# Maxout FFN behind a light convolution: the first blocks' whole-array products reordered, a conv copy moved ahead of a weight copy, three maxima taken in SBUF

## The chip, the cores and the metric

The kernel runs on one core of one Trainium2 chip. The metric is the device time of one execution in microseconds (us), as the median of several runs.

## The reference

Two steps follow each other. The first is a causal depthwise convolution over 7 positions: the 192 channels form 8 heads of 24, each head has its own 7 weights, and these go through a softmax. The second is a maxout feed-forward layer on the 33,280 resulting tokens.

```
w    = softmax(weight, axis=-1)                     # 8 heads x 7
y    = conv over 7 positions, left padded           # (8, 4160, 192) -> 33280 tokens x 192
h    = max(max(y @ w1, y @ w2), y @ w3)             # 33280 x 768
out  = h @ w_out                                    # 33280 x 192
```

## The kernel before

The 33,280 tokens are cut into 65 blocks of 512. A block's hidden layer is worked out in 6 chunks of 128 of the 768 hidden columns. The kernel uses the identity max(a, b, c) = c + max(a - c, b - c, 0): it forms the differences w1 - w3 and w2 - w3 once (`make_wd`, L320, into `wd`), takes `h = max(relu(y @ (w1-w3)), y @ (w2-w3))` for each chunk (`top`, L508 on ScalarE for the relu, L509 on VectorE for the max), and adds y @ (w3 @ w_out) at the end with a product matrix `m16` that is made once from `w3` and `w_out` (`cast_w3`, `transpose_w3`, `make_m`).

A token has 192 values, one and a half times the 128 rows of the matmul array. So each product with a difference matrix is split. The first 128 rows are one whole-array matmul, called F here. The last 64 rows are a half-array matmul, called H; the H of w1 - w3 and that of w2 - w3 stand in the two halves of the array and run side by side. Index 0 and 1 of `wd` hold the first 128 rows of the two differences, index 2 holds the last 64 rows of both, and index 3 (`cross_wd`, L331) holds copies of rows in the other half, for the form that all blocks from block 2 on use (`l1`, L521). For index 2 the last 64 rows of `w3` are needed in both halves of the partitions. They are loaded into the lower half (L244) and copied to the upper one (`copy_w3`, L324).

The weights arrive in DMAs on SyncE's queue, in three groups of 256 columns, that is two chunks each: `load_wa` (L229) brings the first 128 rows of w3, w1 and w2, `load_wb` (L233) the last 64 rows. Behind them come w_out and the inputs of blocks 2 to 6 (`load_x`, L167). Some input buffers are zeroed in part beforehand (`zero_x`, L140 on ScalarE, L137 on GpSimd or VectorE).

Blocks 0 to 3 have a conv of their own (`conv_dense`, matmuls at L396): two PSUM tiles per block, one for the 128 rows that F reads and one for the 64 rows (in both halves) that H reads, each copied to SBUF at L401 by the engine that the call names. `order=(1, 0)` works out the H tile first.

Blocks 0 and 1 run their chunks in pairs: `l1_dense` (L544) issues the F and H matmuls of two chunks, `tops` the maxima. The string "FH" or "HF" gives the order. Block 0 uses the PSUM pools `psp` and `psq` (tiles `lp` and `lq`, two banks each), block 1 uses `psw` (tiles `lw`, four banks). All engines work their instructions off in the order of the program, and a manual schedule fixes that order. `h` of block 0 then goes into the output product (`first_hidden`, L616; `first_rest`, L624 and L629; copies at L632), block 2's conv follows with its copies of halves (`cross`, L407), and from block 2 on a steady pattern interleaves `l1` (L521), the output product `st2` (L585) and the convs of later blocks.

The relus and their copies are in tiles `r` of the pool `rp` (4 buffers before).

Of the kernel before, what the change touches and what calls it, by code (L numbers as in the profile page):

```python
# [10 lines left out]
FP32 = mybir.dt.float32  # L11
FP16 = mybir.dt.float16
# [3 lines left out]
P = 128  # L16
# [5 lines left out]
NBLK = 512  # L22
CHK = 103
HALF = P // 2
# [4 lines left out]
def kernel(  # L29
# [12 lines left out]
    nc = tc.nc  # L42
    ctx.enter_context(tc.manual_schedule())

    B, SEQ, D = x.shape
    H, KWs = weight.shape
# [55 lines left out]
    ysp = ctx.enter_context(tc.tile_pool(name="ysp", bufs=2))  # L102
    ydp = ctx.enter_context(tc.tile_pool(name="ydp", bufs=4))
    ypp = ctx.enter_context(tc.tile_pool(name="ypp", bufs=5))
    rp = ctx.enter_context(tc.tile_pool(name="rp", bufs=4))
    hp = ctx.enter_context(tc.tile_pool(name="hp", bufs=2))
    tp = ctx.enter_context(tc.tile_pool(name="tp", bufs=2))
    outp = ctx.enter_context(tc.tile_pool(name="outp", bufs=3))
# [12 lines left out]
    def get_x(t):  # L121

        if not 0 <= t < NB or t in xin:
            return
        if t < XBUF:
            xbuf.append(const.tile([P, NR, D], FP32, name=f"xf_{t}"))
        xf = xbuf[t % XBUF if t < NDENSE + XBUF else NDENSE + (t - NDENSE - XBUF) % 3]
        assert all(v[0] is not xf for v in xin.values())
        xin[t] = [xf, 0, ()]

    def zero_x(t, q0=0, q1=NR, eng=None):

        if t >= NDENSE:
            get_x(t)
        xf = xbuf[t]
        if eng is not None:
            eng.memset(xf[TOK:HALF, q0:q1, :], 0.0)  # L137
            return
        zero = idle[TOK:HALF, 0:D]
        nc.scalar.copy(out=xf[TOK:HALF, q0:q1, :],  # L140
                       in_=bass.AP(tensor=zero.tensor, offset=zero.offset,
                                   ap=[list(zero.ap[0]), [0, q1 - q0], [1, D]]))
# [59 lines left out]
    NC, NSLOT, CYC = D // HALF, D // 32, 96  # L202
# [21 lines left out]
    ws, w3s = wall[:, 0:NC, :], wall[:, NC:NC + 2, :]  # L224
    PW = 2 * P

    def load_wa(f):
        for st, n, wsrc in ((w3s, 0, moe_w3), (ws, 0, moe_w1), (ws, 1, moe_w2)):
            nc.sync.dma_start(out=st[:, n, f], in_=wsrc[0:P, f])  # L229

    def load_wb(f):
        for st, lo, n, wsrc in ((ws, 0, 2, moe_w1), (ws, HALF, 2, moe_w2)):
            nc.sync.dma_start(out=st[lo:lo + HALF, n, f], in_=wsrc[P:D, f])  # L233

    wk = const.tile([NHEAD, SMALL], FP32, name="wk")[:, 0:KW]
# [5 lines left out]
    load_x(0)  # L241
    load_x(1)
    load_wa(slice(0, PW))
    nc.sync.dma_start(out=w3s[0:HALF, 1, :], in_=moe_w3[P:D, :])  # L244
    load_wb(slice(0, PW))
    for t in range(2, NDENSE):
        get_x(t)
# [39 lines left out]
    for lo, hi, copy in ((0, CUT, nc.scalar.copy), (CUT, WIN, nc.vector.tensor_copy)):  # L287
        bps = psq.tile([32, hi - lo + 3, NHEAD], FP32, tag="q", name=f"band_{lo}")
        for c in range(lo, hi):

            nc.tensor.matmul(bps[:, c - lo:c - lo + 4, :].rearrange("p c h -> p (c h)"),
                             lhsT=line[:, WIN - 1 - c:WIN + 31 - c],
                             rhs=ident16[:, 0:4 * NHEAD], start=True, stop=True)
        bands_.append((lo, hi, copy, bps))
    keep_warm((NBLK, NBLK, P), psp, "p")
    for h0, h1 in ((5, NHEAD), (0, 5)):
        for lo, hi, copy, bps in bands_:
            for a in range(4):
                copy(out=band[32 * a:32 * a + 32, h0:h1, 32 * a + lo:32 * a + hi],
                     in_=bps[:, 0:hi - lo, h0:h1].rearrange("p c h -> p h c"))  # L300
# [12 lines left out]
    wd = const.tile([P, NC + 1, DFF], FP16)  # L313
# [4 lines left out]
    def make_wd(n, j0, j1, eng=nc.vector):  # L318
        f = slice(P * j0, P * j1)
        eng.tensor_sub(out=wd[:, n, f], in0=ws[:, n, f], in1=w3s[:, n // 2, f])  # L320

    def copy_w3(copy, j0, j1):
        f = slice(P * j0, P * j1)
        copy(out=w3s[HALF:P, 1, f], in_=w3s[0:HALF, 1, f])  # L324
# [35 lines left out]
    dense, hs, outs, halves, convs, done = {}, {}, {}, {}, {}, {}  # L360
# [23 lines left out]
    def conv_dense(t, copies, pools=((None, None),) * 2, order=(0, 1)):  # L384


        yd = dense[t] = ydp.tile([P, NC, NBLK], FP16, tag="yd", name=f"yd_{t}")
        for n in order:
            slots_ = ((0, 1, 2, 3), (4, 5, 4, 5))[n]
            pool, tag = pools[n]  # L390
            ps = (pool or psw).tile([P, NBLK], FP32, tag=tag or "w", name=f"D{n}_{t}")
            for (q, b, row_lo, rlen, lo, hi, cc) in chunks_of[t]:
                for v in range(2):
                    for g, s in enumerate(slots_):
                        h = (32 * s + 31 * v) // GRP
                        nc.tensor.matmul(  # L396
                            ps[32 * g:32 * g + 32, lo:hi],
                            lhsT=xz[t][v][0:rlen, q, 32 * s:32 * s + 32],
                            rhs=band[0:rlen, h, cc:cc + hi - lo],
                            start=(v == 0), stop=(v == 1), tile_position=(0, 32 * g))  # L400
            copies[n](out=yd[:, 2 * n, :], in_=ps[:])  # L401
# [46 lines left out]
    def y_row(t, i):  # L448
        return dense[t][HALF * i:HALF * (i + 1), 0, 0, 0, 0, :]

    def y_all(t, i, c):
        if t < NDENSE:
            return dense[t][HALF * i:HALF * (i + 1), side(i, c), :]
        a = y_row(t, i)
        s0, s1, s2, s3 = (spot(t, i, c, r) for r in range(4))
        assert s3 - s2 == s1 - s0
        return bass.AP(tensor=a.tensor, offset=a.offset + P * s0,
                       ap=[list(a.ap[0]), [P * (s2 - s0), 2], [P * (s1 - s0), 2], [1, P]])
# [42 lines left out]
        assert not ops  # L501
        clock[0] = clock[1] = 0

    def top(t, j, ps):
        if t not in hs:
            hs[t] = hp.tile([P, NJ, NBLK], FP16, tag="h", name=f"h_{t}")
        r = rp.tile([P, NBLK], FP16, tag="r", name=f"r_{t}_{j}")
        nc.scalar.activation(out=r[:], in_=ps[0][:], func=AF.Relu)  # L508
        nc.vector.tensor_max(out=hs[t][:, j, :], in0=r[:], in1=ps[1][:])  # L509
        done[t] = j + 1  # L510

    def l1(t, j, pools=((psp, "p"), (psq, "q"))):
# [18 lines left out]
    def l1_dense(tiles, parts="FH"):  # L531

        meet()
        for n, part in enumerate(parts):
            for t, j, pools in tiles:
                for i, (pool, tag) in enumerate(pools):
                    if (t, j, i) not in open_ps:
                        open_ps[t, j, i] = pool.tile([P, NBLK], FP32, tag=tag, name=f"l{tag}{i}_{t}_{j}")
                        begun.discard((t, j, i))
                    if part == "F":  # L540
                        a, b = wd[:, i, P * j:P * (j + 1)], dense[t][:, 0, :]
                    else:
                        a, b = w_of(i, NC - 1, j), y_all(t, i, NC - 1)
                    nc.tensor.matmul(open_ps[t, j, i][:], lhsT=a, rhs=b,  # L544
                                     start=(t, j, i) not in begun, stop=(t, j, i) in begun)
                    begun.add((t, j, i))

    def tops(*tiles):
        for t, j in tiles:
            top(t, j, (open_ps[t, j, 0], open_ps[t, j, 1]))  # L550

    open_ps, begun = {}, set()

# [143 lines left out]
    zero_x(5, eng=nc.gpsimd)  # L697
    make_wd(0, 0, 2)
    make_wd(1, 0, 2)
    copy_w3(ACT, 0, 2)  # L700
    make_wd(2, 0, 2)
    conv_dense(1, (DVE, ACT), order=(1, 0))
    copy_w3(ACT, 2, 6)
    for n in range(NC):
        make_wd(n, 2, 4, nc.gpsimd)
    for n in range(NC):
        make_wd(n, 4, 6, nc.gpsimd)
    cast_w3(0, 6)
    GP(out=wo[:], in_=wos[:])
    l1_dense([(0, 0, PQ), (0, 1, PQ)], "F")  # L710
    l1_dense([(0, 0, PQ), (0, 1, PQ)], "H")
    tops((0, 0), (0, 1))
    l1_dense([(1, 0, WW), (1, 1, WW)], "HF")
    tops((1, 0), (1, 1))
    zero_x(6)
    for t in range(NDENSE, XBUF):
        load_x(t)
    l1_dense([(0, 2, PQ), (0, 3, PQ)], "FH")
    tops((0, 2), (0, 3))
    l1_dense([(1, 2, WW), (1, 3, WW)], "HF")  # L720
    tops((1, 2), (1, 3))
    cross_wd(0, ACT)
    l1_dense([(0, 4, PQ), (0, 5, PQ)], "FH")
    tops((0, 4), (0, 5))
    cast_dense(2, (GP, GP))
# [1 line left out]
    tops((1, 4), (1, 5))  # L727
    transpose_w3((PQ[0], PQ[0], PQ[1]))
    cast_dense(3, (GP, GP))
    cross_wd(1, ACT)  # L730
    first_hidden(0)
    first_hidden(1)
# [118 lines left out]
```

## Time and profile before

| | before |
|---|---|
| median of 3 runs | 452.76 us (452.75 to 453.1) |
| profiled execution, its own time | 454.16 us |
| its span, first to last instruction | 452.40 us |
| PE busy | 445.5 us (98%) |
| VectorE (DVE) busy | 354.6 us (78%) |
| ScalarE (ACT) busy | 320.2 us (71%) |
| GpSimd (POOL) busy | 207.6 us (46%) |
| granted TensorE clock | 1.00 |

Busy time is a mean over stages that have different limits, so the table says only that PE is the busiest. The change touches the first 25 us alone; its cost has to be read from that stretch: which wait ends last in front of PE, and how long the stretch is up to the point from which PE never waits again. PE is matmuls, PEld weight loads into the array, SP (or SPq) SyncE's queue. An entry in brackets behind a row is the idle time of that engine just before it, and what released it.

### The profile page before, as it was taken

How to read it: one execution, taken by the hardware profiler on the slowest of the kernel's cores; microseconds unless marked ns; L12 is line 12 of the kernel's file. 1: busy time of each engine (PE TensorE's matmuls, PEld its weight loads, DVE VectorE, ACT ScalarE, POOL GpSimd, SP SyncE). 2: the span in 40 equal slices, each digit the busy share in tenths (PEclk: the TensorE clock that was granted, in tenths of full speed). 3: DMA queues.
4: the chain of work that ended last, by engine and by line, in shares of the span. 5: the costliest groups of instructions: out<-in, count | busy, mean ns of one | idle time of the engine just before them, and what ended most of it. 6: DMA issues, size and time to landing. Idle time of an engine off the chain costs nothing.

```text
span 452.4 us, 18264 instructions
## 1 busy us (share of the span) xinstructions
PE 445.5 (98%) x7576; PEld 409.8 (91%) x7576; DVE 354.6 (78%) x607; ACT 320.2 (71%) x601; POOL 207.6 (46%) x239
## 2 busy tenths in 40 slices
PE   7999999999999999999999999999999999999997
PEld 4469999999999989999999999999999999999996
DVE  6668787878878787787887787887887887887775
ACT  6967767767777677676676776777776776776664
POOL 5864836556463533724824635525533644224000
PEclk9999999999999999999999999999999999999999
DMA  7968987696885659649649748657649668152123
GB/s 197 239 181 167 203 186 197 155 217 171 170 220 147 165 137 205 162 121 199 167 127 198 178 110 191 191 114 193 178 112 197 172 157 143 54 136 75 58 71 106
DMA packets 128163, 72.01 MB, mean 159 GB/s; under 512 B 52305, under 2 KB 127888, under 8 KB 128080
## 3 DMA queue, kind: packets, MB, share of 16 engines
q1 hardware_dynamic: 127919, 70.75, 65.9%
q8 instruction: 59, 0.97, 0.9%
q14 instruction: 25, 0.20, 0.2%
q10 hardware_dynamic: 160, 0.10, 0.1%
HBM read 33.28 MB, written 25.56 MB: 130 GB/s over the span
## 4 chain that ended last, share of the span: by engine, by line
PE 96%; DMA 1%; ACT 1%; SPq 1%; issue 1%; DVE 0%; ACTq 0%
PE po L585 36%; PE lq L521 32%; PE lp L521 22%; PE G L375 3%; DMA wall<-in_moe_w_dram 1%; ACT r L508 1%; PE D L396 1%; PE po L643 0%; PE po L616 0%; PE lw L544 0%; SPq L229 0%; SPq L167 0%; PE pm L355 0%; ACT wall L324 0%; PE lq L544 0%
## 5 line engine op out<-in xcount | busy, mean ns | idle before, releaser
L585 PE MATMUL po<-wo,h 64*128 64x192 f16 x3024 | 331.7, 243 | 0.0
L509 DVE TENSOR_TENSOR h<-r,lq 128x512 f16<-128x512 f16 x384 | 263.0, 686 | 86.2 <-ACT r L508 76.3
L508 ACT ACTIVATE r<-lp 128x512 f16<-128x512 f32 x384 | 228.9, 597 | 113.8 <-PE lp L521 103.0
L521 PE MATMUL lp<-yp,wd 64*128 64x512 f16 x1098 | 295.6, 376 | 0.0
L521 PE MATMUL lq<-yp,wd 64*128 64x512 f16 x1098 | 295.5, 376 | 0.0
L585 PEld LDWEIGHTS <-h 64*128 64x128 f16 x3024 | 242.7, 94 | 5.4 <-issue 4.1
L521 PEld LDWEIGHTS <-wd 64*128 64x128 f16 x2268 | 181.7, 94 | 14.8 <-issue 0.2
L199 POOL CAST x<-xf 103x768 f16<-103x768 f32 x122 | 97.3, 825 | 114.4 <-DMA xf<-in_x_dram 99.6
L585 PE MATMUL po<-m,yp 64*128 64x192 f16 x720 | 140.3, 243 | 0.0
L438 POOL COPY yp<-yp 64x1536 f16<-64x1536 f16 (+1 forms) x70 | 90.9, 1298 | 86.0 <-DMA yp<-ys 49.1
L593 DVE TENSOR_TENSOR o<-a,po 128x384 f32<-128x384 f32 x126 | 69.0, 547 | 0.0
L585 PEld LDWEIGHTS <-yp 64*128 64x128 f16 x720 | 66.3, 94 | 0.1
L592 ACT COPY a<-po 128x384 f32<-128x384 f32 x126 | 59.6, 473 | 0.0
L415 ACT CAST ys<-G 128x480 f16<-128x480 f32 (+1 forms) x53 | 25.4, 530 | 9.5 <-PE G L375 9.2
L415 DVE CAST ys<-G 128x480 f16<-128x480 f32 (+1 forms) x53 | 30.1, 610 | 0.0
L375 PE MATMUL G<-x,band 39*32 39x240 f16 (+3 forms) x1024 | 16.5, 242 | 0.0
L375 PEld LDWEIGHTS <-band 39*32 39x32 f16 x1024 | 10.2, 92 | 4.6 <-issue 4.1
L521 PE MATMUL lq<-yd,wd 64*128 64x512 f16 x36 | 9.7, 376 | 0.0
L521 PE MATMUL lp<-yd,wd 64*128 64x512 f16 x36 | 9.7, 376 | 0.0
L544 PEld LDWEIGHTS <-wd 128*128 128x128 f16 (+1 forms) x48 | 3.0, 95 | 7.3 <-issue 1.7
L396 PEld LDWEIGHTS <-xz 112*32 112x32 f16 x320 | 4.1, 96 | 2.9 <-issue 1.4
L216 POOL CAST xz<-xf 112x160 f16<-112x160 f32 (+2 forms) x18 | 5.1, 328 | 3.2 <-DMA xf<-in_x_dram 3.0
(75 smaller groups left out, 100.0 us busy)
## 6 DMA issues: line engine op xcount, KB each, us to landing
xf<-in_x_dram SPq DMA_DIRECT2D x113, 234.0 KB
out_dram<-o SPq DMA_DIRECT2D x62, 384.0 KB
xf<-in_x_dram SPq DMA_DIRECT2D x7, 204.8 KB
wall<-in_moe_w_dram SPq DMA_DIRECT2D x11, 128.0 KB
xf<-in_x_dram SPq DMA_DIRECT2D x3, 420.0 KB
yp<-ys SPq DMA_TRANSPOSE x70
out_dram<-o SPq DMA_DIRECT2D x5, 192.0 KB
wos<-in_moe_w_out_dram SPq DMA_DIRECT2D x1, 576.0 KB
```

The lines of the kernel that those rows point to most:

```text
L199: nc.gpsimd.tensor_copy(out=x16s[t0][0:K, :, :, u, r, :].rearrange("p h j c -> p j h c"), in_=xf[0:K, 4 * r:4 * r + 4, :].rearrange("p j ( ...
L216: copy(out=xz[t][v][0:rl, q0:q1, :].rearrange("p q (k c) -> p q k c", c=CYC)[:, :, :, a:b], in_=xf[0:rl, q0:q1, :].rearrange("p q (k c) -> ...
L375: nc.tensor.matmul(G[2 * (k // per) + i][TOK * j:TOK * (j + 1), k % per, :], lhsT=band[row, h, HALF * i + LAP:HALF * i + KR], rhs=x16s[t0] ...
L396: nc.tensor.matmul(ps[32 * g:32 * g + 32, lo:hi], lhsT=xz[t][v][0:rlen, q, 32 * s:32 * s + 32], rhs=band[0:rlen, h, cc:cc + hi - lo], star ...
L415: copy(out=slots[t][:, i % 2, :, :, GRP * h0:GRP * (h0 + per)].rearrange("p u r (h c) -> p h (u r) c", c=GRP), in_=G[i][:].rearrange("p h ...
L438: nc.gpsimd.tensor_copy(out=yp[HALF * i:HALF * (i + 1), 1, :, :, :, :].rearrange("p i u k n -> p (i u k n)"), in_=yp[HALF * (1 - i):HALF * ...
L508: nc.scalar.activation(out=r[:], in_=ps[0][:], func=AF.Relu)
L509: nc.vector.tensor_max(out=hs[t][:, j, :], in0=r[:], in1=ps[1][:])
L521: nc.tensor.matmul(ps[i][:], lhsT=w_of(i, c, j), rhs=y_all(t, i, c), start=(n == 0), stop=(n == NC - 1))
L585: nc.tensor.matmul(ps[b0, i][:, s % 2, :], lhsT=a, rhs=b, start=first, stop=last)
L592: nc.scalar.copy(out=a[:], in_=ps[s - 1, 0][:])
L593: nc.vector.tensor_add(out=outs[t][:, s - 1:s + 1, :], in0=a[:], in1=ps[s - 1, 1][:])
```

## The change

- `l1_dense` with "F" takes the two chunks' products with w1 - w3 first and those with w2 - w3 after them. The order within "H" stays.
- In the first pair of chunks the order is now F of block 0, F of block 1, H of block 0 and its maxima, H of block 1 and its maxima. Before it was F and H of block 0 with its maxima, then H and F of block 1 with its maxima. The other pairs keep their order.
- Block 1's conv copies change engines: the H tile is copied by VectorE and the F tile by ScalarE. ScalarE's weight copy of chunks 0 and 1 stands behind that copy.
- The last 64 rows of w3 are loaded in the two pieces of `load_wb` (columns 0 to 255, and 256 to 767) instead of one load for all columns ahead of it.
- The weight copy of chunks 2 to 5, one instruction on ScalarE before, is split: chunks 2 and 3 on GpSimd, chunks 4 and 5 on ScalarE behind the first pair's maxima.
- The difference `wd[0]` of chunks 2 and 3 moves from GpSimd to VectorE.
- The zeroing of buffer 6 moves from ScalarE, behind the first pair's maxima, to GpSimd, ahead of the differences.
- In block 1's chunks 1, 3 and 5 ScalarE copies the second product from PSUM to an f16 tile of `rp`, and VectorE's max reads that instead of PSUM.
- `cross_wd(0)` moves from behind the second pair to behind `transpose_w3`, next to `cross_wd(1)`.
- `rp` has 5 buffers.

```diff
-    rp = ctx.enter_context(tc.tile_pool(name="rp", bufs=4))
+    rp = ctx.enter_context(tc.tile_pool(name="rp", bufs=5))
...
     def load_wb(f):
-        for st, lo, n, wsrc in ((ws, 0, 2, moe_w1), (ws, HALF, 2, moe_w2)):
+        for st, lo, n, wsrc in ((w3s, 0, 1, moe_w3), (ws, 0, 2, moe_w1), (ws, HALF, 2, moe_w2)):
...
     load_wa(slice(0, PW))
-    nc.sync.dma_start(out=w3s[0:HALF, 1, :], in_=moe_w3[P:D, :])
     load_wb(slice(0, PW))
...
-    def top(t, j, ps):
+    def top(t, j, ps, spare=False):
...
-        nc.vector.tensor_max(out=hs[t][:, j, :], in0=r[:], in1=ps[1][:])
+        q = ps[1]
+        if spare:
+            q = rp.tile([P, NBLK], FP16, tag="r", name=f"q_{t}_{j}")
+            nc.scalar.copy(out=q[:], in_=ps[1][:])
+        nc.vector.tensor_max(out=hs[t][:, j, :], in0=r[:], in1=q[:])
...
-        for n, part in enumerate(parts):
-            for t, j, pools in tiles:
-                for i, (pool, tag) in enumerate(pools):
...
+        for part in parts:
+            order = [(i, v) for i in range(2) for v in tiles] if part == "F" else [(i, v) for v in tiles for i in range(2)]
+            for i, (t, j, pools) in order:
...
-            top(t, j, (open_ps[t, j, 0], open_ps[t, j, 1]))
+            top(t, j, (open_ps[t, j, 0], open_ps[t, j, 1]), t == 1 and j % 2 == 1)
...
+    conv_dense(1, (ACT, DVE), order=(1, 0))
     copy_w3(ACT, 0, 2)
     make_wd(2, 0, 2)
-    conv_dense(1, (DVE, ACT), order=(1, 0))
-    copy_w3(ACT, 2, 6)
-    for n in range(NC):
-        make_wd(n, 2, 4, nc.gpsimd)
+    make_wd(0, 2, 4)
+    zero_x(6, eng=nc.gpsimd)
+    make_wd(1, 2, 4, nc.gpsimd)
+    copy_w3(GP, 2, 4)
+    make_wd(2, 2, 4, nc.gpsimd)
+    l1_dense([(0, 0, PQ), (0, 1, PQ)], "F")
+    l1_dense([(1, 0, WW), (1, 1, WW)], "F")
+    l1_dense([(0, 0, PQ), (0, 1, PQ)], "H")
+    tops((0, 0), (0, 1))
+    l1_dense([(1, 0, WW), (1, 1, WW)], "H")
+    tops((1, 0), (1, 1))
+    copy_w3(ACT, 4, 6)
     for n in range(NC):
         make_wd(n, 4, 6, nc.gpsimd)
     cast_w3(0, 6)
     GP(out=wo[:], in_=wos[:])
-    l1_dense([(0, 0, PQ), (0, 1, PQ)], "F")
-    l1_dense([(0, 0, PQ), (0, 1, PQ)], "H")
-    tops((0, 0), (0, 1))
-    l1_dense([(1, 0, WW), (1, 1, WW)], "HF")
-    tops((1, 0), (1, 1))
-    zero_x(6)
...
     tops((1, 2), (1, 3))
-    cross_wd(0, ACT)
...
     cast_dense(3, (GP, GP))
+    cross_wd(0, ACT)
     cross_wd(1, ACT)
```

More of the change, by code (lines that the diff above doesn't have):

```diff
@@ L533, in l1_dense @@
         meet()
-        for n, part in enumerate(parts):
-            for t, j, pools in tiles:
-                for i, (pool, tag) in enumerate(pools):
[L537 to L546, printed above, removed]
+        for part in parts:
+            order = [(i, v) for i in range(2) for v in tiles] if part == "F" else [(i, v) for v in tiles for i in range(2)]
+            for i, (t, j, pools) in order:
+                pool, tag = pools[i]
+                if (t, j, i) not in open_ps:
+                    open_ps[t, j, i] = pool.tile([P, NBLK], FP32, tag=tag, name=f"l{tag}{i}_{t}_{j}")
+                    begun.discard((t, j, i))
+                if part == "F":
+                    a, b = wd[:, i, P * j:P * (j + 1)], dense[t][:, 0, :]
+                else:
+                    a, b = w_of(i, NC - 1, j), y_all(t, i, NC - 1)
+                nc.tensor.matmul(open_ps[t, j, i][:], lhsT=a, rhs=b,
+                                 start=(t, j, i) not in begun, stop=(t, j, i) in begun)
+                begun.add((t, j, i))
     def tops(*tiles):
         for t, j in tiles:
-            top(t, j, (open_ps[t, j, 0], open_ps[t, j, 1]))
+            top(t, j, (open_ps[t, j, 0], open_ps[t, j, 1]), t == 1 and j % 2 == 1)
     open_ps, begun = {}, set()
```

## The prediction

> **What bounds the kernel now.** I read the table of stages first (engine busy time in chosen stretches; the columns after the times are PE, PEld, DVE, ACT and POOL busy with instruction counts, then granted clock, DMA share, GB/s).
>
> ```profile
> 8.94:12.91 3.97, 2.88 (x24) 1.10 (x17) 1.83 (x5) 2.97 (x6) 2.30 (x4) 1.00 0.67 195
> 12.91:15.88 2.97, 2.97 (x17) 1.01 (x16) 1.86 (x4) 2.92 (x5) 1.61 (x3) 1.00 0.89 269
> 15.88:19.47 3.59, 3.35 (x18) 1.00 (x16) 3.26 (x6) 3.56 (x7) 3.50 (x4) 1.00 1.06 238
> 31.00:440.00 409.00, 408.98 (x6922) 385.25 (x6920) 327.66 (x545) 290.48 (x545) 185.85 (x196) 1.00 0.67 157
> ```
>
> From 31 to 440 us PE is busy for 408.98 of 409.00 us, at clock 1.00: time saved ahead of that is time saved at the end, and nothing else is to be had there. The three rows above it are the three pairs of chunks (0,1), (2,3), (4,5) of blocks 0 and 1, which the change reorders: 10.53 us together. Their matmuls are 24 F at a start-to-start step of 0.216 us and 12 pairs of H at the same step, 36 x 0.216 = 7.78 us; the other 2.75 us are waits and turns from F to H, so the change can win 2.7 us at the very most. Then the chain that ended last, for its first 30 us:
>
> ```profile
> 3.71 6.13 DMA wall<-in_moe_w_dram
> 9.86 0.40 ACT wall L324
> 10.29 0.58 ACT yd L401
> 10.90 0.62 ACT wall L324
> 11.54 1.38 ACT r L508 x3
> ...
> 13.63 0.68 ACT xf L140
> ...
> 15.75 0.70 DVE h L509
> 16.45 0.04 issue
> 16.49 0.38 PE lq L544
> ...
> 27.88 0.84 issue
> ```
>
> Until 16.49 the path is ScalarE's queue, after a weight load that landed at 9.84; from there it is PE, apart from 0.84 us in the middle of block 3's conv, where PE waited for nothing that the profile shows. Last, two queues in order of time (start, length, engine, line, work, and in brackets idle time and its releaser):
>
> ```profile
> 8.21 1.37 POOL L137 MEMSET xf<- 32x1536 f32 x1
> 10.92 1.41 POOL L320 TENSOR_TENSOR wd<-wall 128x256 f16<-128x256 f32 x2 [1.34 <-DMA wall<-in_moe_w_dram]
> 12.66 0.73 POOL L320 TENSOR_TENSOR wd<-wall 128x256 f16<-128x256 f32 x1 [0.33 <-ACT r L508]
> 13.71 0.72 POOL L320 TENSOR_TENSOR wd<-wall 128x256 f16<-128x256 f32 x1 [0.33 <-DMA wall<-in_moe_w_dram]
> 15.47 1.42 POOL L320 TENSOR_TENSOR wd<-wall 128x256 f16<-128x256 f32 x2 [1.03 <-DMA wall<-in_moe_w_dram]
> ```
>
> ```profile
> 8.17 1.23 SPq L233 DMA_DIRECT2D wall<-in_moe_w_dram  x1
> 9.45 0.60 SPq L233 DMA_DIRECT2D wall<-in_moe_w_dram  x1
> ```
>
> POOL's last weight difference, wd[2] of chunks 4 and 5, ends at 16.89 (15.47 + 1.42) and waited for a landing: this is a floor that no order on PE or ScalarE moves.
>
> **Part 1: the first pair.** Before, F of block 0 starts at 8.94 and ends at 9.82 (4 x 0.216); then PE idles until H at 11.06, since wd[2] waits for the weights and for ScalarE's copy (9.86). Now ScalarE's first work is block 1's conv copy (0.58, conv ended about 9.0), DVE takes the other half (0.69), and F of block 1 fills 9.82 to 10.68. The load ahead of the wd[2] weights shrinks from 192 to 64 KB; at the 195 GB/s of this stage 128 KB are 0.66 us, so they land near 9.7 and not at 10.4. ScalarE's weight copy (0.40) follows the conv copy at 9.65, the subtraction (0.42) ends near 10.5, and H can start at 10.8, 0.26 earlier; H of block 1 follows directly. The first relu starts 0.48 after H, at 11.3 instead of 11.54. If the landing doesn't move, H starts at 11.06 as before and the gain here is nothing.
>
> **Part 2: ScalarE's account.** Taken away: the zeroing of buffer 6 (1.47, L140) and the second weight copy of 0.62, of which 0.40 come back (chunks 4 and 5) behind the first maxima. Added: three copies of 128x512 out of PSUM. The nearest row is L401, 0.585 each; relus in a row start 0.49 apart (11.54, 12.03), so 1.47 to 1.76 together; I take 1.47, as they stand in rows of relus. Sum: -1.47 - 0.62 + 0.40 + 1.47 = -0.22 us, at worst +0.07. The engine is not relieved; work is moved from where it stalls PE to where it may not. The copy of wd across halves (0.83, L331) leaves 17.21 and goes behind the w3t copies.
>
> **Part 3: the other queues.** POOL gets the zeroing (1.37, same shape as its row at 8.21) exactly in its idle 1.34 us before 10.92; if that cover went, wd[1] of chunks 2 and 3 would come up to 1.37 late. It also gets one 64x256 weight copy: between 0.25 (its smallest L216 cast) and 0.73 (L320), I take 0.40, the ScalarE row for this shape; it gives one subtraction (0.70 start to start) to DVE, where it costs 0.42. That subtraction waits for a load on DVE, and four maxima queue behind it; it would end at 11.34 if the load lands as before, while the first max needs its relu (11.3 + 0.6), so 0.5 us hide it. The three maxima from SBUF cost between 0.25 (half of L407's 0.50, a 512-element f16 copy within SBUF) and the 0.68 of the maxima as they are, and I take 0.50; DVE has room (1.86 busy of 2.97), so this is no term. The F order and the fifth r buffer: nothing. SP issues one DMA more, 0.33 to 0.60 ahead of the last weights.
>
> **Part 4: where it ends.** Pair 2: H needs wd[2] of chunks 2 and 3, POOL's at 13.39, unmoved, so H stays at 13.87; but the relu that was ready 0.44 later (14.31) began at 15.12, behind the zeroing; now ScalarE is free at 11.3 + 5 x 0.49 + 0.43 = 14.2. 0.8 us are won here. Pair 3: PE is through with pair 2 at about 15.5, and H of chunks 4 and 5 then waits for the floor: 16.89 + 0.1 = 17.0 instead of 17.40. Of 0.8 us 0.4 are left. From there ScalarE: relu at 17.55, four relus and a copy to 20.1, w3t copies (1.56) to 21.67, now both wd copies (1.66) to 23.3, then block 2's conv copy, which before began at 22.90 after waiting 0.37 for PE. So ScalarE is 0.4 late for that copy; the copy of halves behind it (0.62) ends at 24.55, and the third matmul of chunk 0 of block 2, at 24.83 before, starts at 24.6. With unmoved landings PE gains 0.25 us.
>
> **Part 5: the landings.** The 1.23 us issue at 8.17 stands against 0.60 of its twin, while SP's queue was held behind loads in flight; with 128 KB less ahead it may fall to 0.60 and everything behind it lands up to 0.6 earlier; the extra issue gives 0.33 to 0.60 back. So the last weights come between 0.6 earlier and 0.6 later. PE's own earlier progress pulls at the first end: a 16 KB packet of its code ran from 13.20 for 0.93 us in the DMA records, on one of the engines that carried the last weights, and most of that load's packets were through by then; PE passes that point of its program about 1 us earlier now. I take 0.3 earlier. Sum: -0.25 - 0.3 = -0.55 us. The profiled execution took 454.16 (span 452.40, 1.76 around it), 1.40 above the median of 452.76; 453.6 for it, 452.2 for the median. A difference of 0.2% (0.9 us) is about what a measurement of this kernel can tell from no change, so this forecast lies within it: 0.52.
>
> **Rivals.** *The last weights land a whole microsecond earlier* (for it: POOL waits 1.34 us before 10.92 and 1.03 before 15.47 for weights alone; against: SP's extra issue). Then wd[2] ends near 16.0, and ScalarE alone bounds: 11.3 + 7.4 (12 relus, 3 copies) + 0.43 + 1.56 + 1.66 = 22.3, with about 0.4 of waits in between 22.7, so block 2's third matmul at 23.9 and up to 0.9 saved there; with a code wait shorter than 0.84 at 27.88 about 1.1 in all: 451.6. Chance of over 0.9 faster: 0.31.
>
> *ScalarE takes PE's place as the bound* (slower). If the last weights come 0.5 us late, relu at 17.95 as before, one more copy (0.49) and the moved one (0.83) put the conv copy of block 2 at 24.0, 1.1 late; m16 and the relu of block 2 follow on the same queue, and DVE's copy of block 0's output behind that relu frees the bank of block 3's conv (27.39 before) 1.05 late. That gives +1.05: 453.8. It decides from about 15.9 for the landing. For it: ScalarE is busy 3.56 of 3.59 us; against: it idles 2.1 us at 28. Chance of over 0.9 slower: 0.17.
>
> *DVE and POOL hold each other up.* The first trace has them only 0.09 us side by side with two SBUF operands each (DVE to 11.01, POOL from 10.92), with no stretch. If they exclude each other, DVE's new subtraction and the max of chunk 1 (0.42 + 0.5) push POOL's wd up to 0.9 late, but POOL's waits for landings (0.33 and 1.03) hide all of it but 0.3: 452.5, within the same 0.52. The Trainium skill, "SBUF — State Buffer", section "Who interferes with whom", states such a rule: a VectorE instruction with two SBUF inputs and a GpSimd one that reads SBUF shut each other out. The 0.09 us of the trace are too short to bear it out or not.
>
> *The code wait at 27.88 grows by what was won*: 452.8, also within 0.52.
>
> **Range.** 451.2 to 453.5: from the faster rival with its landing 0.4 earlier still, to two thirds of the slower one.
>
> **What would show it.** Right: F of block 1 before 10.8, no ScalarE zeroing at 13.6, the third pair's H at 16.6 to 17.0, ScalarE without a gap up to block 2's conv copy, and that copy no earlier than 22.6. Wrong: wd[2] of chunks 4 and 5 after 17.3; the conv copy after 23.7 with PE idle at L521; POOL's L320 longer than 0.73; or a PE gap after 31 us.

## The result and the profile after

The changed kernel is slower. Its median is 454.60 us over 22 runs, that of the kernel before on the same chip 453.17 us over 22 runs; the ratio is 1.0031, with a 95% interval from 1.0017 to 1.0044, so about 1.4 us more. The forecast was 0.55 us less.

Two things have to be known to read the profile. The execution that was profiled after took 454.13 us (span 452.34), 0.47 below its median; the one before took 454.16 (span 452.38), 0.99 above the median of its 22 runs. So the two traces have the same length though the medians are 1.4 us apart, and no single pair of traces can hold the whole loss. And the line numbers have moved: by one down to the relu (the m copy is L356 now, the conv copy L400, the relu L507), by 3 to 4 behind it (the max is L512, `l1` L524, `l1_dense` L548). The new copy is L511.

First the stages of the changed kernel, in the same columns as before: the three pairs, the stretch from their end to block 2's first product, and the steady part.

```profile
9.58:12.49 2.91, 2.88 (x24) 1.11 (x18) 1.49 (x4) 1.64 (x4) 2.00 (x4) 1.00 0.75 204
12.49:15.96 3.47, 3.13 (x17) 1.00 (x16) 3.03 (x5) 3.42 (x8) 2.16 (x4) 1.00 0.92 268
15.96:18.95 2.99, 2.96 (x17) 1.01 (x16) 2.80 (x6) 2.83 (x6) 2.99 (x3) 1.00 1.05 234
18.95:24.79 5.84, 4.95 (x130) 4.57 (x129) 3.04 (x6) 5.74 (x12) 4.79 (x15) 1.00 0.92 206
31.00:440.00 409.00, 408.48 (x6883) 384.38 (x6872) 327.10 (x544) 289.99 (x544) 186.18 (x196) 1.00 0.66 157
```

The three pairs together take 9.37 us where they took 10.53, so the reordering does what it says: 1.16 us are saved in the stage. They begin at 9.58 and not at 8.94 (0.64 lost) and end at 18.95 and not at 19.47. The fourth row is where it goes wrong: PE is busy for 4.95 of 5.84 us there, and ScalarE for 5.74. Before, the stretch from 19.47 to block 2's first product at 24.40 took 4.93 us, all of it PE:

```profile
19.47:24.40 4.93, 4.93 (x129) 4.54 (x128) 2.58 (x5) 4.45 (x9) 4.07 (x14) 1.00 0.90 215
```

The chain of waits of the changed kernel shows the same (start, length, what):

```profile
17.41 0.64 DVE h L512
18.05 0.48 ACT r L507
18.53 0.47 issue
19.00 0.60 ACT r L507
19.60 0.48 ACT q L511
20.08 1.47 ACT w3t L348 x3
21.55 0.03 issue
21.57 0.83 ACT wd L330
22.41 0.02 issue
22.43 0.83 ACT wd L330
23.26 0.02 issue
23.29 0.59 ACT yd L400
...
24.43 0.32 ACT m L356
24.74 0.04 issue
24.79 0.37 PE lp L524
...
32.68 0.49 issue
```

Before, this chain lay on PE from 16.49 on. Now it lies on ScalarE up to 24.74: relus, the third new copy (`q`, L511), the w3t copies, both copies of wd, block 2's conv copy, and the m copy. Ahead of 17.41 it runs back over the relus and copies on ScalarE to 11.85, then over PE's first pair and the casts of block 1's input; the last weights are no link of it. What hands it over to PE are these rows of the timeline (in brackets PE's idle time before it, and its releaser):

```profile
24.43 0.52 ACT L356 CAST m<-pm 128x192 f16<-128x192 f32 x2
24.79 0.37 PE L524 MATMUL lp<-yd,wd 64*128 64x512 f16 x1 [0.89 <-ACT m L356]
```

Block 2's first product doesn't wait for its operands. It waits for a PSUM bank: `psp` has two, the products for m16 hold both, and ScalarE's first m copy gives one back. Before, that copy ended just as PE came:

```profile
24.04 0.72 ACT L357 CAST m<-pm 128x192 f16<-128x192 f32 x2
24.40 0.37 PE L521 MATMUL lp<-yd,wd 64*128 64x512 f16 x1
```

The last row of the chain, 0.49 us of "issue" at 32.68, is a wait that the experiments below put down to PE's own code; before it was 0.84 at 27.88.

The queues that the forecast followed, GpSimd and VectorE (start, length, engine, line, work, idle time and releaser):

```profile
7.06 2.87 POOL L137 MEMSET xf<- 32x1536 f32 x2
14.08 2.27 POOL L319 TENSOR_TENSOR wd<-wall 128x256 f16<-128x256 f32 x3 [1.31 <-DMA wall<-in_moe_w_dram]
```

```profile
6.84 1.77 DVE L216 CAST xz<-xf 112x160 f16<-112x160 f32 x3
```

The last weight difference ends at 14.08 + 2.27 = 16.35, against 16.89 before. The two zeroings ran one behind the other from 7.06, and the casts of block 1's input on VectorE beside them took 1.77 us for three: 0.25 for the first, 1.47 and 1.49 for the two behind it, which began at 7.02 and 7.13 and ended at 8.49 and 8.62, when the first zeroing (1.37 of the 2.87) was just through. That is the late start of F in this trace, and in this one alone. In the other 18 traces that can be read, of both orders, no such cast took over 0.50 us, and F began at 8.57 to 9.49. The zeroing beside the casts is the first one, which the kernel before has too; GpSimd came to it at 7.06 and not 8.21 since its own casts of block 1 were through sooner here.

### The profile page after: what moved, and what is told of

It reads as the page before. It is cut to its first block, busy times and chain, and to the rows that moved or that the text cites. A ratio compares the mean times of both kernels' runs of the same rounds, so it can differ in the third digit from the quotient of the medians.

```text
span 452.3 us, 18266 instructions
## 1 busy us (share of the span) xinstructions
PE 445.2 (98%) x7576; PEld 409.3 (90%) x7576; DVE 356.4 (79%) x608; ACT 320.0 (71%) x603; POOL 209.2 (46%) x240
## 4 chain that ended last, share of the span: by engine, by line
PE 95%; ACT 2%; DMA 1%; issue 1%; DVE 1%; SPq 0%; POOL 0%; ACTq 0%; POOLq 0%
PE po L589 36%; PE lq L524 32%; PE lp L524 22%; PE G L374 3%; ACT r L507 1%; DMA xf<-in_x_dram 1%; PE D L395 0%; PE po L647 0%; ACT wd L330 0%; DVE xz L216 0%; ACT w3t L348 0%; ACT q L511 0%; PE lw L548 0%; PE lp L548 0%; SPq L167 0%
## 5 line engine op out<-in xcount | busy, mean ns | idle before, releaser
L512 DVE TENSOR_TENSOR h<-r,lq 128x512 f16<-128x512 f16 x384 | 263.0, 685 | 86.1 <-ACT r L507 75.6
L507 ACT ACTIVATE r<-lp 128x512 f16<-128x512 f32 x384 | 229.0, 597 | 114.6 <-PE lp L524 103.6
L524 PE MATMUL lp<-yp,wd 64*128 64x512 f16 x1098 | 295.6, 376 | 0.0
L524 PE MATMUL lq<-yp,wd 64*128 64x512 f16 x1098 | 295.6, 376 | 0.0
L524 PEld LDWEIGHTS <-wd 64*128 64x128 f16 x2268 | 181.4, 94 | 15.5 <-issue 1.0
L524 PE MATMUL lp<-yd,wd 64*128 64x512 f16 x36 | 9.7, 376 | 0.9 <-ACT m L356 0.9
L524 PE MATMUL lq<-yd,wd 64*128 64x512 f16 x36 | 9.7, 376 | 0.0
L548 PEld LDWEIGHTS <-wd 128*128 128x128 f16 (+1 forms) x48 | 3.0, 96 | 6.1 <-issue 2.7
```

The source lines that it names most:

```text
L512: nc.vector.tensor_max(out=hs[t][:, j, :], in0=r[:], in1=q[:])
L524: nc.tensor.matmul(ps[i][:], lhsT=w_of(i, c, j), rhs=y_all(t, i, c), start=(n == 0), stop=(n == NC - 1))
```

## The experiments

Four theories were on record by the end. **A**: ScalarE's queue is the path, and the m copy at its end frees the bank too late. **B**: GpSimd's zeroing shuts VectorE's casts out, and the late start is the loss. **C**: the last weights land later. **D**: PE waits for its code behind the input loads, and the clock falls behind that wait. All ratios are to the kernel before on the same chip, with 95% intervals; they can differ from the quotient of two medians by about 0.001. There are 12 executions each unless told. Variants have their lines moved by up to 3.

**The three copies (A).** The changed kernel without them:

```diff
-            top(t, j, (open_ps[t, j, 0], open_ps[t, j, 1]), t == 1 and j % 2 == 1)
+            top(t, j, (open_ps[t, j, 0], open_ps[t, j, 1]))
```

> The changed kernel without the three copies of a second product to SBUF (VectorE's max reads PSUM again). Theory A, ScalarE's queue: its work up to the m16 copy that frees the first product's PSUM bank in block 2 was 0.4 us longer than before and PE waits for it, so 1.47 us less there takes 0.8 to 1.2 us off: 0.2 to 0.6 us above the kernel before, and the m16 copy before 24.0 instead of 24.43. Theory B, GpSimd's zeroing shuts VectorE's casts out: nothing changes, 1.4 us above the kernel before. Theory C, the last weights land later: nothing changes either.

Measured: 453.50, ratio 1.0001 [0.9988, 1.0013]. The loss is gone, but none of the forecast gain is there. The same three copies added to the kernel before (with `rp` of 5):

> The kernel before with one part of the change alone: the three copies of a second product to SBUF, and the fifth r buffer. Theory A, ScalarE's queue: its work up to the m16 copy grows by 1.47 us with no slack but 0.4, so 0.7 to 1.2 us above the kernel before, m16 copy at 25.0 or later instead of 24.04. Rival, the copies free PSUM banks earlier and shorten three maxima: no difference or faster.

Measured: 454.25, ratio 1.0016 [1.0003, 1.0029]: 0.7 us by the ratio. By this measurement the copies cost time where nothing else is changed, but that ScalarE's queue is the reason isn't shown: in the trace PE waited for the cast of w_out, which landed at 20.64.

**The zeroing (B).** The changed kernel with the zeroing of buffer 6 back on ScalarE, behind its weight copy of chunks 4 and 5:

```diff
-    zero_x(6, eng=nc.gpsimd)
...
     copy_w3(ACT, 4, 6)
+    zero_x(6)
```

> The changed kernel with the zeroing of buffer 6 back on ScalarE behind the first pair's maxima, the three copies kept. Theory A: ScalarE has 1.47 us more ahead of block 2, so 2.2 to 2.9 us above the kernel before, m16 copy at 25.5 or later. Theory B: one GpSimd zeroing fewer, but the one that meets VectorE's casts stays: 1.0 to 1.4 us above.

Measured: 454.92, ratio 1.0037 [1.0024, 1.0050]: 1.6 us more, which is neither A's 2.2 to 2.9 nor B's 1.0 to 1.4. Then both kernels with GpSimd held back until VectorE's last cast of block 1 was through (a copy of two elements on GpSimd that reads that cast's output, ahead of `zero_x(5)`):

> The changed kernel with a two-element GpSimd copy ahead of its two zeroings that reads what VectorE's last cast of block 1 writes, so that no zeroing runs beside those casts. Theory A: 1.0 to 1.4 us above the kernel before, as the changed kernel. Theory B: VectorE's casts take 0.25 to 0.5 us each and not 1.47, F of block 0 starts by 9.0 in place of 9.65, and the time is 0.4 to 0.9 us above the kernel before.

> The kernel before with the same two-element copy ahead of its one GpSimd zeroing at that place. Theory A: no difference, within 0.3 us. Theory B: where block 1's input lands early the zeroing meets the casts here too, so 0.3 to 0.7 us below the kernel before on the mean of the runs.

Measured: 1.0029 [1.0010, 1.0048] for the changed kernel, 1.0015 [1.0005, 1.0026] for the kernel before. In the trace of the first F began at 8.78, where it was 8.94 before the change, and the time stayed. B falls as the cause of the loss: the casts are shut out in one trace of the record, and held apart they win nothing. Why the same small copy costs the kernel before 0.15% isn't explained.

**The last weights (C).** No run was made for it, but the traces speak against it. The last weight difference ends at 16.14 to 16.89 in the six traces of the old order, and at 16.12 to 17.31 in twelve of the thirteen of the changed one; in the thirteenth, the changed kernel without copies, it ends at 19.04.

**ScalarE relieved (A).** The changed kernel with both copies of wd on VectorE, the same without the three copies, and the kernel before with its second copy of wd on VectorE:

```diff
-    cross_wd(0, ACT)
-    cross_wd(1, ACT)
+    cross_wd(0, DVE)
+    cross_wd(1, DVE)
```

> The changed kernel, its three copies kept, with both copies of the differences across halves on VectorE (idle there for 2.2 us) in place of ScalarE, so 1.66 us fewer in ScalarE's queue. Theory A: m16 copy before 24.0, 0.8 to 1.3 us off the changed kernel: 0.1 to 0.6 above the kernel before. Rival, the copies cost by something else than ScalarE's queue: still 1.2 to 1.5 above.

> The changed kernel without the three copies and with both copies across halves on VectorE: ScalarE has 3.1 us fewer. Theory A: ScalarE no longer bounds; what is late next is block 2's conv, whose input GpSimd casts until about 21.3 or later, so 0.3 to 0.8 us below the kernel before. Rival: as e1, no difference from the kernel before.

> The kernel before with its second copy across halves on VectorE: 0.83 us fewer for ScalarE just ahead of block 2's conv copy, which waited 0.37 us for PE before. Theory A: m16 copy 0.3 to 0.4 us earlier, and the time 0 to 0.4 us below the kernel before. Rival, VectorE's copy shuts GpSimd's casts out and block 2's conv comes later: 0.3 to 0.8 above.

Measured: 1.0029 [1.0013, 1.0045], 1.0023 [1.0007, 1.0040] and 1.0001 [0.9989, 1.0013]. This speaks against A as the whole cause: 1.7 us are taken off ScalarE, and the median doesn't move. The traces of the first two show that the stage itself did get shorter (the table below).

**More copies, and the bank freed earlier (A).** The copy in all six chunks of block 1, and the first m copy moved ahead of the copy of halves:

```diff
-            top(t, j, (open_ps[t, j, 0], open_ps[t, j, 1]), t == 1 and j % 2 == 1)
+            top(t, j, (open_ps[t, j, 0], open_ps[t, j, 1]), t == 1)
```

> The changed kernel with the ScalarE copy in front of the maximum in all six chunks of block 1 instead of three (three copies of 128x512 more, rp of 6 buffers). Theory A (ScalarE's queue is the path from 11.8 us to the bank of block 2's first product, so each copy counts in full): 3 x 0.49 = +1.5 us on the changed kernel, block 2's conv copy at 24.8 and not 23.3, about 456.0, ratio to the kernel before near 1.006. Theory D (the loss is a wait for PE's code and the clock behind it, the copies only move where PE stands when the packets come): no more than 0.5 us on the changed kernel, ratio 1.002 to 1.004.

```diff
+    make_m(0)
     cast_x(4)
     cross(2, ACT, DVE)
-    make_m(0)
     make_m(1)
```

> The changed kernel, with the first m copy (0.26 us) ahead of the copy across halves (0.62) on ScalarE. Theory A (PE's first product of block 2 waits for the bank that the m copy frees): first product at 24.2 and not 24.79, but the third then waits for the copy across halves to 24.8 instead of 25.0: 0.2 us less than the changed kernel, ratio 1.0025. Theory D: the 0.2 us are lost in the next wait for code, ratio 1.003.

> The changed kernel without its three ScalarE copies and with the first m copy ahead of the copy across halves: the version that could beat both. Theory A: 0.2 us less than the changed kernel without the copies, ratio to the kernel before 0.9995. Theory D: the same as that one, 1.000, give or take the waits for code.

Measured: 1.0031 [1.0015, 1.0047] with six copies, 1.0019 [1.0002, 1.0036] with the m copy first, and 1.0018 [1.0001, 1.0036] with that and no copies. Six cost what three cost, so a plain sum over ScalarE's queue doesn't give the median. No version beat the kernel before.

What these edits do to the stage can be read without the noise of the medians. The table gives, for each trace, the start of the third pair's first relu, the start of block 2's first product, and the time between them.

| kernel | first relu of pair 3 | block 2's first product | between |
|---|---|---|---|
| before | 17.95 | 24.40 | 6.45 |
| before, second wd copy on VectorE | 17.32 | 23.78 | 6.46 |
| after | 17.54 | 24.79 | 7.25 |
| after, zeroing 6 on ScalarE | 18.35 | 25.60 | 7.25 |
| after, GpSimd held back | 16.85 | 24.09 | 7.24 |
| after, six copies | 18.44 | 26.23 | 7.79 |
| after, no copies | 19.52 | 26.38 | 6.86 |
| after, m copy first | 17.35 | 23.96 | 6.61 |
| after, both wd copies on VectorE | 18.08 | 24.44 | 6.36 |
| after, that and no copies | 17.85 | 24.33 | 6.48 |
| after, m copy first and no copies | 17.30 | 23.59 | 6.29 |

The last column hardly moves between traces of the same order on ScalarE: 6.45 or 6.46 in four traces of the old one, 7.24 or 7.25 in five of the new one (those not listed are the late load and the loads left out, below). Two traces of the old order fall out of it, with PE as the bound: 7.59 where GpSimd was held back (the output product began at 20.60), and 7.44 where the copies were added (w_out landed at 20.64 and the cast of it let PE go on at 21.89). The change adds 0.80 us to this stretch, and the sum over ScalarE's rows says why: 0.97 and 0.97 for four relus, 0.47 for the copy, 1.62 for w3t, 1.72 for two copies of wd, 0.61 for the conv copy, 0.53 for the copy of halves, 0.36 for the m copy, 7.25 us in all. The copy and one copy of wd, 0.47 + 0.86 = 1.33, are new in it; without them ScalarE would need 5.92, and PE's own path took 6.45. So 0.53 of the 1.33 are hidden, and 0.80 are not. The two columns to the left move by up to 2.8 us from trace to trace. Part of that is when the last weights land (without copies), part what stands ahead of the third pair (six copies, the zeroing on ScalarE). It is the noise in which the medians lie.

**The input loads (D).** The load of buffer 6 moved from the others (12 to 20 us) to behind the load of block 7, in both kernels:

```diff
-    for t in range(NDENSE, XBUF):
+    for t in range(NDENSE, XBUF - 1):
         load_x(t)
...
     load_x(7)
+    load_x(6)
     cast_x(5)
```

> The changed kernel, with the load of buffer 6 (192 KB and more, issued among the loads of 4 and 5 at 12 to 20 us) issued behind the load of block 7, at about 27 us; its cast to f16 starts at 30 us. Theory D (input loads fill the DMA engines from 12 to 27 us, hold up PE's code packets, and the wait costs PE its clock): no gap of PE at 27 to 33 us, no run near 456.5, so about 0.5 to 1.0 us less than the changed kernel: 453.7 to 454.1, ratio 1.001 to 1.002. Theory A (ScalarE's queue): unchanged, ratio 1.003. If the late load holds up its cast and the conv of block 7 behind it, slower.

> The kernel before with the same later load of buffer 6. Theory D: the wait of 0.84 us at 27.88 goes, 0.5 to 0.8 us less than the kernel before: ratio 0.998 to 0.999. Theory A: ratio 1.000.

Measured: 1.0064 [1.0040, 1.0088] (8 executions) for the changed kernel, 1.0025 [1.0006, 1.0043] for the kernel before. The opposite of what D expected, and yet it shows D's mechanism. PE's rows of the changed kernel with the late load, and the granted clock in two stretches of the kernel before with the late load (columns as in the table of stages):

```profile
31.55 0.24 PE L589 MATMUL po<-wo,h 64*128 64x192 f16 x1
34.26 0.34 PE L589 MATMUL po<-wo,h 64*128 64x192 f16 x4 [2.46 <-issue]
```

```profile
31.00:34.30 3.30, 1.09 (x18) 0.67 (x15) 1.52 (x3) 0.77 (x2) 1.56 (x3) 0.91 0.89 263
34.30:38.00 3.70, 3.70 (x38) 3.10 (x39) 0.96 (x2) 1.18 (x3) 1.57 (x3) 0.62 1.18 132
```

In both traces PE waits over 2 us at the same instruction of its program (2.46 and 2.21), for nothing but issue: the 224th matmul behind the last product for m16. The waits of 0.84 us before and 0.49 after stand at the 96th and the 224th. In the DMA records PE's fourth packet of code (16 KB) starts 8.05 and 7.68 us after block 2's first product (at 31.95 and 31.84); in 13 traces with the load at its old place it starts 4.2 to 7.0 us after it. The late load filled the DMA engines from 27 us on, just when this packet was due (DMA share 0.97 and 0.94 from 27 to 32 us, 0.60 in the kernel before). Seven traces have a wait of 0.49 us or more at one of the two instructions, and in each PE goes on 1.2 to 1.5 us after the end of the third or fourth packet: that is why the waits are put down to code. In the kernel before the clock is then at 0.62 over the next 3.7 us; in the changed kernel it stayed at 1.00 in the same stretch, so such a wait doesn't always bring the clock down.

The same happened without that edit, in the changed kernel with both wd copies on VectorE:

```profile
27.90:29.90 2.00, 0.02 (x1) 0.00 (x0) 0.49 (x1) 0.35 (x1) 1.51 (x4) 1.00 0.97 289
29.90:33.40 3.50, 3.48 (x43) 2.29 (x44) 1.55 (x3) 0.75 (x2) 1.42 (x2) 0.56 0.27 79
```

PE stands still for 2.0 us in the middle of block 3's conv while the DMA share is 0.97, and then works for 3.5 us at a clock of 0.56. From block 2's first product to the last matmul this trace has 427.44 us, traces without a code wait 423.76 to 424.15: 3.3 to 3.7 us lost by one late packet (the third here, which starts at 27.26; in the trace of after it starts at 25.22). The changed kernel with the m copy first and no copies waited at the same place:

```profile
27.40:29.50 2.10, 0.04 (x5) 0.02 (x7) 0.32 (x1) 0.18 (x1) 1.91 (x4) 1.00 0.92 275
29.50:33.00 3.50, 3.50 (x43) 2.41 (x44) 1.38 (x3) 0.60 (x1) 1.32 (x2) 0.51 0.18 47
```

Executions with such a stretch can be told without a trace, since their mean clock is 0.996, as in the three traces that have one: 19 of 118 of the kernels with the changed order and all loads at their old place, against 2 of 193 of those with the old order. (The 22 executions of the kernel before in the first measurement have no clock on record; two of them, 456.69 and 456.88, are as long.)

Then the input loads of blocks 5 and 6 left out (their casts read block 4's buffer), in the changed kernel, the kernel before, and the changed kernel without copies:

```diff
         xf = xin[t][0]
+        if t in (5, 6):
+            xin[t] = [xbuf[4], xin[4][1], xin[4][2]]
+            return
```

> The changed kernel with the input loads of blocks 5 and 6 left out (their casts read block 4's buffer; every other instruction stays): the DMA engines carry a third of the input traffic between 12 and 27 us. Theory D (the loss against the kernel before is waits of PE for its code behind those loads, with the lower clock that follows): no PE gap between 25 and 35 us, no run at a mean clock of 0.996, and the time is the same as that of the kernel before with the same loads left out, to 0.3 us, or less than it. Theory A (ScalarE's queue with the three copies): 0.4 to 1.4 us more than that kernel.

> The kernel before with the same loads of blocks 5 and 6 left out: the twin of the run above. Theory D: its wait of 0.84 us at 27.88 goes, 0.5 to 0.8 us less than the kernel before, ratio 0.998 to 0.999. Theory A: the same as before, ratio 1.000.

> The changed kernel without its three ScalarE copies, and with the same loads of blocks 5 and 6 left out. Theory A: 1.0 to 1.5 us less than the changed kernel with these loads left out (3 x 0.49 on the path). Theory D: at most 0.4 us less.

Measured: 454.34, ratio 1.0020 [1.0008, 1.0032]; 453.20, ratio 0.9988 [0.9970, 1.0006]; 453.41, ratio 0.9999 [0.9985, 1.0013]. By these, the changed kernel is still 1.1 us longer than its twin, and 0.9 of it are the three copies. What the DMA engines carry between 12 and 27 us falls by a quarter, from 3.27 MB to 2.47 in the kernel before and from 3.12 to 2.36 in the changed one. But the first of them didn't repeat:

> The changed kernel with the input loads of blocks 5 and 6 left out, once more: the first profile of it was taken while the granted clock had fallen away, so its stages could not be read. Theory A (ScalarE's queue): ScalarE without a gap from 11.8 us to block 2's conv copy, that copy at 23.3 or later against 22.70 in the twin of the kernel before, and about 0.9 us more than that twin. Theory D (code waits): PE gaps between 25 and 35 us that the twin does not have.

> The same kernel with the last of the three copies (chunk 5 of block 1) left out, the copies of chunks 1 and 3 kept. Theory A, with the first two copies ended before ScalarE has to wait for the third pair's products at 17.5 us: the last copy alone is on the path, 0.5 us less than with three. If all three count, 0.3 less; if it is not ScalarE's queue, no difference.

Measured: 453.45, ratio 1.0000 [0.9990, 1.0010], on another chip of the same kind, and with two copies 453.65, ratio 1.0015 [1.0000, 1.0030]. The two measurements of one kernel, 1.0020 and 1.0000, lie outside each other's intervals. So differences of 0.2% between two measurements aren't settled by these intervals, and the difference to the twin without the loads is anything from 0.2 to 1.1 us by the medians, 0.5 to 1.5 by the ratios. With two copies the median isn't below that with three.

The traces without the loads are clean, but for the first of the changed kernel, which is of an execution of 2,626 us and can't be read. None of the other four (the kernel before, the changed one, the changed one without copies and with two) has a PE wait for code after 26 us; from block 2's first product to the last matmul they have 424.03, 423.79, 423.74 and 423.75 us. PE's fourth packet of code starts 4.3 to 4.6 us after block 2's first product in all four, where it was 4.2 to 7.0 with the loads: the loads can hold the code up. Of the executions with the changed order 2 of 47 have a mean clock of 0.996, where it was 19 of 118 with the loads. And the stretch of the table is the same as with the loads: 6.46 for the kernel before, 7.25 for the changed one; with the last copy alone left out 6.86, as without all three with the loads (6.98 without loads and copies). So of the three copies the last alone is in this stretch, 0.39 us of it, as theory A expected of the trace.

## Why the prediction was wrong

**Part 4 failed, in its last step.** The first links are close: the third pair's H was forecast at 17.0 and stands at 17.11, its relu at 17.55 and stands at 17.54, and block 2's conv copy was forecast at 23.3 and stands at 23.29. The first of these is luck: H was to follow the last weight difference, which was through at 16.35, and it was PE, still busy with the pair's F products, that held it to 17.11. Then the text said that the third matmul of chunk 0 of block 2 starts at 24.6 and PE gains 0.25 us. It starts at 25.21, 0.38 later than before. The forecast followed the operand (the copy of halves, forecast to end at 24.55, ended at 24.52) and not the bank: the m copies stand behind that copy on ScalarE, and the first product needs what they free. In the trace of before that row was there, the m copy at 24.04 and the product at 24.40, with no wait showing since PE came just then. A link without slack was taken for one without weight. With the m copy moved ahead of the copy of halves the stretch is 6.61 and not 7.25, which shows the step; how much of the 1.4 us it is stays open (below).

**The slower rival had the right engine and the wrong condition.** *ScalarE takes PE's place as the bound* was made to depend on weights that land after 15.9 and late. The last difference ended at 16.35, 0.54 earlier than before, and ScalarE was the bound all the same. Its price, 1.05, was worked out for that late landing; the stretch is 0.80 longer whenever the landing comes.

**Part 2's sum was right and its use wrong.** ScalarE's busy time of the page is 320.0 us against 320.2, which is the forecast -0.22. "Work is moved from where it stalls PE to where it may not" is the sentence that failed: it went behind the third pair's first relu, and there 1.33 us met 0.53 us of slack.

**Part 1.** F of block 1 was forecast from 9.82 to 10.68 and ran from 10.46; H was forecast at 10.8 and began at 11.41, the first relu at 11.84 and not 11.3. The pair itself was right: H stands 1.83 us behind F of block 0, forecast 1.86. What failed is the start of F, taken as 8.94 and 9.58 here: the first zeroing on GpSimd (from 7.06 on; before, from 8.21) stood beside VectorE's casts, and two casts stood still for its length. The rival on this named the subtraction and the maxima and not the casts. The Trainium skill, "SBUF — State Buffer", section "Who interferes with whom", says that a VectorE copy or cast in a two-port mode and GpSimd lock each other out for a whole instruction; the casts of 1.47 and 1.49 us beside the first zeroing agree, against the 0.25 of the one ahead of it. Held apart, the kernel was no faster. Nor does the forecast gain of 0.26 show in the other traces: H began at 10.47 to 11.41 in thirteen of the changed order, at 10.38 to 11.06 in six of the old.

**Part 3.** The weight copy on GpSimd was taken at 0.40 and took 0.47, the zeroing at 1.37 and both together took 2.87. The maxima out of SBUF were taken at 0.50 and took 0.54 to 0.67, against 0.68 out of PSUM. All three stand beside GpSimd instructions that read SBUF. In the trace without the loads one has GpSimd idle beside it (first row); in that with GpSimd held back one began beside GpSimd's cast of w3 and ended behind it (the others):

```profile
13.86 0.43 DVE L515 TENSOR_TENSOR h<-r,q 128x512 f16<-128x512 f16 x1
```

```profile
16.32 1.46 POOL L327 CAST w3h<-wall 128x1536 f16<-128x1536 f32 x1
16.61 1.44 DVE L512 TENSOR_TENSOR h<-r,q 128x512 f16<-128x512 f16 x1
```

So the hold-up that the rival on VectorE and GpSimd supposed is there in the maxima too. That it costs time isn't shown: the stretch is 7.24 or 7.25 in both traces, as after.

**Part 5.** The last weights were forecast 0.3 earlier and their difference ended 0.54 earlier in this trace. The issue that was to fall from 1.23 to 0.60 took 1.25 us; the reason given failed, and the direction held by luck: over the traces the difference ends no earlier (theory C above).

**The code wait.** The rival put it down as a wait that grows by what was won, which would end at no change. It is worse than that: the time lost is drawn anew in each execution, and in the changed order the long draw with the low clock comes in 16% of them (19 of 118) and not in 1%. At about 2 us more each that is 0.3 us of the mean, by estimate.

**The signs.** Most signs of "right" came, though the time went the other way: F of block 1 before 10.8, no zeroing on ScalarE, its queue nearly without a gap, the conv copy at 23.29. None of them looks at the bank. Two signs of "wrong" came: one of GpSimd's differences took 0.91 us, and PE has a gap after 31 us (0.49 at 32.68).

**What stays open.** The stretch is 0.80 us longer, and the experiments show why. That this is what the medians lost is not shown. The third pair's first relu starts 0.35 earlier (17.26 on average over six traces of the changed order with three copies, without that with the zeroing on ScalarE; 17.61 over five of the old order). With 0.3 for the low clock this makes an estimate of about 0.75 us, and 1.4 was measured. Read directly the traces show less: block 2's first product starts at 24.28 on average in four traces of the changed order (after, GpSimd held back, the late load, loads left out) and at 24.29 in five of the old one. But six of the seven traces with three copies are of executions faster than the median of their kernel, by up to 1.96 us, so they may not hold what a usual execution loses. The low clock isn't the rest: without its three executions at 0.996 the changed kernel's median is still 454.31.

The edits that bring the stretch back to 6.3 to 6.6 us don't bring the median back (1.0018 to 1.0029), and leaving the copies out does in one form (1.0001) and not in two others (1.0023 and 1.0018). Why the changed order meets the late code packets more often was not found; that the input loads have a part in it is what the runs without them suggest (2 of 47).

## What to carry to other kernels

Work taken from one stall must be followed to the next point where it has no slack: here 1.33 us of copies came to stand behind the third pair's first relu, and what went beyond 0.53 us of slack was paid in that stretch. When an engine's first instruction of a stage is costed, list its output buffer with its operands, and see who frees it and what stands ahead of that on its queue. Where two medians are 0.3% apart and landings move a stage by more than that from run to run, measure the stretch between two points behind the landing instead: it repeated to 0.01 us in nine traces, while two medians of one kernel lay 0.9 us apart. But a stretch is not the time: edits that made this one short again left the median where it was.

## What the runs showed of the hardware

- PE waits when the 16 KB packets of its code come late: waits of 0.49 to 2.46 us at two fixed instructions, 128 matmuls apart, in seven traces, ended 1.2 to 1.5 us after such a packet. With a load issued just ahead the fourth packet started 7.7 to 8.1 us after block 2's first product, with two loads fewer 4.3 to 4.6. Moving one load by some 10 us moved the wait and made both kernels slower by about 0.3% (from 1.0031 to 1.0064, and to 1.0025).
- A wait of 2.0 us was followed by 3.5 us at a granted clock of 0.56, one of 2.06 by 3.5 us at 0.51, one of 2.21 by 3.7 us at 0.62, one of 2.46 by none. The Trainium skill, "TensorE: Matmul & The Clock Gate", section "Part 1: The HAM clock gate (the "warmup" mystery)", puts the fall of the clock after an idle window of about 3.4 us; here shorter idle times than that were enough. That the low clock lasts for about one such window agrees.
- A max of two 512-wide f16 operands in SBUF took 0.42 or 0.43 us with GpSimd idle beside it, against 0.68 with one operand in PSUM. Beside GpSimd's cast of w3 one took 1.44 us and ended 0.27 after that cast.
- VectorE's f32 to f16 casts of 0.25 to 0.50 us took 1.47 and 1.49 beside a GpSimd memset of 1.37, in the one trace where they met.
